# Windowed attention and an MLP on one core: both score tiles of a pair moved next to another pair's value products, five PSUM banks shared in turn

## The chip, the cores and the metric

One core of a Trainium2 chip runs the whole program in one launch. The metric is device time in microseconds (us) of one execution; a profiled execution also leaves a trace of every instruction on TensorE (PE, with its weight loads as PEld), VectorE (DVE), ScalarE (ACT), GpSimd (POOL) and the DMA queues.

## The reference

The inputs have batch 2, 8 heads, 768 positions and head dimension 64. Attention keeps the first four keys and a window of 128; its output feeds an MLP (512 to 2048 to 512) with a clipped quadratic gate; a last stage adds experts for tokens whose score is positive.

```
scores = scale * np.matmul(q, k.transpose(0, 1, 3, 2))
keep = is_sink | in_window
scores = np.where(keep, scores, -1000000000.0)
a = np.exp(scores - np.max(scores, axis=-1, keepdims=True))
a = a / (np.sum(a, axis=-1, keepdims=True) + 1e-09)
x = np.matmul(a, v)            # then heads side by side: 1536 tokens x 512
h = x @ w_in                   # float64 weights
g = np.where(h >= 1, h, np.where(h <= -1, 0.0, (h + 1) ** 2 / 4))
y = g @ w_out
```

## The kernel before

**Work.** A unit is one head over 256 queries (two tiles of 128); two heads make a pair, so there are 48 units and 24 pairs, 12 per batch. A pair goes through these steps, each with its engine:

- `trans_q`, `trans_k` (lines 304, 331): PE transposes of queries and keys into one bank each, which ACT copies out (lines 307, 334; in batch 1 lines 310, 336, and DVE then subtracts for a low part).
- `score(u, t)` (line 366): for query tile t the products of both heads. Each head has 64 rows, so the two heads lie in the upper and the lower half of the array (the trace writes 64*128) and run at the same time. Batch 0 has one part in full precision, batch 1 three parts in a faster format. Then per head DVE adds the mask and takes the maximum (line 370, `negmax`), which frees the bank, and ACT takes the exponential (line 374).
- `norm(u)` (lines 381 to 400): POOL, a reciprocal on DVE, four scalings (ACT for the first seven pairs, line 389, DVE after, line 391), small copies on POOL.
- `ptrans(n)` (line 417): PE transposes of one unit's weights, copied out by ACT (`pth`, line 421); `ptrans_sinks(u)` (line 429) for the four sink keys (`psk`, line 430).
- `av(u)` (lines 443, 446): the value products; each head writes 64 columns (128*64 in the trace), the sinks go first in the full array. ACT and DVE copy them out as `xh` and `xl` (lines 451, 452).

**The MLP between them.** From step 10 on, "pieces" of the MLP's first part fill PE between the attention steps: a piece is six matmuls of `h_mm` (line 467, tile `ph`) or three of `y_mm` (line 529, tile `y`). One unit of the MLP is four `h` pieces into one bank `ph`, of which there is only one. When its last piece is done, ACT takes a Relu (line 481) and a Square (line 482), DVE a minimum (line 487), which frees the bank, then ACT writes `gh` (line 489) and DVE `gl` (line 495). Between the last `h` piece of a unit and the first of the next, two `y` pieces stand. The last `y` of a group also has a copy out (`mr`, ACT line 554 and DVE line 552).

**Order.** PE's order is written by hand: for each step `s_` a string is read letter by letter. `a` and `b` are a pair's first and second score tile (`b` also the norm), `q` and `k` the transposes, `P` and `s` the transposes of weights and sinks, `A` the value products, and each dot a share of the step's pieces (three pieces a step). A period of two steps handles one pair. The other engines' order is chosen when the program is built; each works strictly in that order.

**Banks.** PSUM has eight: two for `y`, one for `ph`, two for score tiles (`pss`) and three (`pst`) in turn for transposes and value products. In the second half of the program (`behind`) the MLP alone remains.

Of the kernel before, what the change touches and what calls it, by code (L numbers as in the profile page):

```python
# [8 lines left out]
F32 = mybir.dt.float32  # L9
# [6 lines left out]
PSUM = bass.MemoryType.PSUM  # L16
# [8 lines left out]
def attention_moe_skip_kernel(  # L25
# [19 lines left out]
    P = 128  # L45
# [18 lines left out]
    psy = ctx.enter_context(tc.tile_pool(name="psy", bufs=1, space=PSUM))  # L64
    psh = ctx.enter_context(tc.tile_pool(name="psh", bufs=1, space=PSUM))
    pctx = ctx.enter_context(ExitStack())
    pss = pctx.enter_context(tc.tile_pool(name="pss", bufs=2, space=PSUM))
    pst = pctx.enter_context(tc.tile_pool(name="pst", bufs=3, space=PSUM))
    psz = None


# [27 lines left out]
    for i in range(2):  # L99
        a, b = mask[i][:, 0:P], mask[i][:, P + SK:]  # L100
# [166 lines left out]
    NPR = NU // 2  # L267
    natqk, pr_ = {}, [dict() for _ in range(NPR)]

    def geo(n):  # L270

        b, g, h = units[n]
        return b, g, h, ([2 * g + 1, 2 * g] if g % 2 else [2 * g, 2 * g + 1]), (0 if g % 2 else 1)
# [66 lines left out]
    def span_of(n, t):  # L340

        g = units[n][1]
        if g == 0:
            return (P + SK, P, first) if t == 0 else (P + SK, W, early)
        return ((t + g) % 2) * (P + SK), W, mask[g % 2]

    def score(u, t):

        b, g, h, _, _ = geo(2 * u)
        qt = pr_[u]["qt"]  # L350
        if t == 0:
            pr_[u].update(pr=ap.tile([P, 2, 2, W], F32, name="pr", bufs=2), lsum=ap.tile([P, 4], F32, name="lsum", bufs=2))
        pr, lsum = pr_[u]["pr"], pr_[u]["lsum"]
        c0, w, m = span_of(2 * u, t)
        scs = [pss.tile([P, 512], F32, name="sc") for j in range(2)]
        q_, k_ = slice(P * t, P * t + P), slice(c0, c0 + w)
        if b == 0:
            kt = ktf[h // 2]
            parts = [(qt[:, q_], kt[:, k_])]
        else:  # L360
            kt = kts[h // 2]
            parts = [(qt[:, x, q_], kt[:, y, k_]) for x, y in ((0, 0), (0, 1), (1, 0))]
        for n, (qq, kk) in enumerate(parts):
            for j in range(2):
                r = slice(D * j, D * j + D)
                nc.tensor.matmul(scs[j][:, :w], qq[r], kk[r], start=(n == 0), stop=(n == len(parts) - 1))  # L366
        for j in range(2):
            mi = (b * H + h + j) * (S // P) + 2 * g + t
            a = pr[:, j, t, :w]
            nc.vector.tensor_tensor_reduce(  # L370
                out=a, in0=scs[j][:, :w], in1=m, scale=-0.125, scalar=BIG,
                op0=ALU.add, op1=ALU.min, accum_out=negmax[:, mi:mi + 1],
            )
            nc.scalar.activation(  # L374
                a, a, AF.Exp, bias=negmax[:, mi:mi + 1], scale=-1.0, accum_out=lsum[:, 2 * j + t:2 * j + t + 1])

    def norm(u):
        g = units[2 * u][1]
        pr, lsum = pr_[u]["pr"], pr_[u]["lsum"]
        rs = ap.tile([P, 4], F32, name="rs", bufs=2)  # L380
        nc.gpsimd.tensor_scalar(out=rs, in0=lsum, scalar1=1e-9, scalar2=None, op0=ALU.add)
        nc.vector.reciprocal(rs, rs)
        for j in range(2):
            for t in range(2):
                w = span_of(2 * u, t)[1]
                a, r = pr[:, j, t, :w], rs[:, 2 * j + t:2 * j + t + 1]
                if u < 7:

                    nc.scalar.activation(a, a, AF.Copy, scale=r)  # L389
                else:  # L390
                    nc.vector.tensor_scalar(out=a, in0=a, scalar1=r, scalar2=None, op0=ALU.mult)
        if g:

            pc = pcs[u % 2]
            for j in range(2):
                c = SK * j
                dst = pc.rearrange("p t (x c) -> p t x c", x=9)[:, :, 0::8, c:c + SK]
                src = pr[:, j, :, P:P + SK]
                nc.gpsimd.tensor_copy(dst, src.unsqueeze(2).to_broadcast([P, 2, 2, SK]))
                nc.gpsimd.tensor_tensor(  # L400
                    out=pc[:, :, 32 + c:32 + c + SK], in0=src, in1=pc[:, :, c:c + SK].bitcast(F32), op=ALU.subtract)
# [280 lines left out]
    def prepare(s_):  # L682

        un = (s_ + 1) // 2 + 2
        upto("qk", un // 2 + 2, NU // 4, load_qk)
        if s_ >= 0:
            upto("v", (s_ // 2 + 1) // 2 + 1, NU // 4, load_v)
        return un
# [12 lines left out]
    with tc.manual_schedule(engines={mybir.EngineType.PE}):  # L701
        for s_ in range(-1, NU + 1):
            un = prepare(s_)
            before = done["p"]
            if s_ == -1:
                for t in ktf:
                    nc.gpsimd.tensor_copy(t[:, P + SK + P:2 * (P + SK)], zero[:, 0:SK])
                for t in kts:
                    nc.gpsimd.tensor_copy(t[:, :, P + SK + P:2 * (P + SK)], zero[:, 0:SK].unsqueeze(1).to_broadcast([P, 2, SK]))
                for t in pcs:  # L710
                    nc.gpsimd.memset(t.bitcast(F32), 0.0)
            if s_ == 3:
                raw_to(2)
                sinks(0)
            if s_ == NU // B + 3:
                sinks(1)
            np_ = npieces[s_] if s_ >= 0 else 0
            if s_ >= 0:
                convert_to(conv_for(sum(npieces[:s_ + 5])))
            if s_ < 0:  # L720
                for u in range(un - 1):
                    trans_q(u)
                    trans_k(u)
                done["tq"] = done["tk"] = un - 1
                score(0, 0)

            order = ("aAPs", "bqkAPs", "..a..A...Ps", "..b.qk.APs.")[s_ % 2 + 2 * (s_ >= 9)]
            dots, dot = order.count("."), 0
            for what in order:
                if what == ".":  # L730
                    a, b = np_ * dot // dots, np_ * (dot + 1) // dots
                    dot += 1
                    for i in range(b - a):
                        pieces[done["piece"]]()
                        done["piece"] += 1
                elif what == "q":
                    upto("tq", done["tq"] + 1, NPR, trans_q)
                elif what == "k":
                    upto("tk", done["tk"] + 1, NPR, trans_k)
                elif what == "a" and s_ // 2 + 1 < NPR:  # L740
                    score(s_ // 2 + 1, 0)
                elif what == "b" and (s_ + 1) // 2 < NPR:
                    score((s_ + 1) // 2, 1)
                    norm((s_ + 1) // 2)
                elif what == "P":
                    upto("p", s_ + (s_ >= LAG), NU, ptrans)
                elif what == "s":
                    upto("ps", (s_ + (s_ >= LAG)) // 2, NPR, ptrans_sinks)
                elif what == "A":
                    upto("av", before // 2, NPR, av)  # L750

        bad = const.tile([P, 1], F32, name="bad")
        ext = const.tile([P, 4], U32, name="ext")
        nc.sync.dma_start(ext[:, 0:2], n_sink.bitcast(U32).unsqueeze(0).to_broadcast([P, 2]))
        nc.sync.dma_start(ext[:, 2:4], window.bitcast(U32).unsqueeze(0).to_broadcast([P, 2]))
        extf = const.tile([P, 4], F32, name="extf")
        nc.vector.tensor_copy(extf, ext)
        sel = const.tile([P, 6], F32, name="sel")
        for i, val in enumerate((SK, 0, P, 0)):
            nc.vector.tensor_scalar(out=sel[:, i:i + 1], in0=extf[:, i:i + 1], scalar1=float(val), scalar2=None, op0=ALU.not_equal)  # L760
        nc.vector.tensor_reduce(out=bad, in_=negmax, axis=AX.X, op=ALU.max)
        nc.vector.tensor_scalar(out=sel[:, 4:5], in0=bad, scalar1=1.0e8, scalar2=None, op0=ALU.is_gt)
        actx.close()
        pctx.close()
        pst = ctx.enter_context(tc.tile_pool(name="pst1", bufs=1, space=PSUM))
        zctx = ctx.enter_context(ExitStack())
        psz = zctx.enter_context(tc.tile_pool(name="psz", bufs=1, space=PSUM))
        wp2 = wctx.enter_context(tc.tile_pool(name="wp2", bufs=8))
        wsk = wp2.tile([P, DM], F32, name="wsk", bufs=1)
        nc.sync.dma_start(wsk, w_skip.unsqueeze(0).to_broadcast([P, DM]))  # L770

        E_ = mybir.EngineType
        with tc.manual_schedule(engines={E_.DVE, E_.Activation, E_.Pool, E_.SP}):
            behind()
# [3 lines left out]
    pss = ctx.enter_context(tc.tile_pool(name="pss1", bufs=2, space=PSUM))  # L778
# [270 lines left out]
```

## Time and profile before

| what | us |
|---|---|
| median of three runs | 413.43 (411.69 to 414.58) |
| the profiled execution: its own time | 414.2 |
| the profiled execution: span of the trace | 412.4 |
| PE busy, share of the span | 382.7, 93% |
| DVE busy | 256.0, 62% |
| ACT busy | 221.1, 54% |

The page is read in three stretches: up to about 58 us the attention alone, then to about 216 us attention with pieces of the MLP between, then the MLP alone. The profiled execution is 0.77 us above the median.

### The profile page before, as it was taken

How to read it: one execution, taken by the hardware profiler on the slowest of the kernel's cores; microseconds unless marked ns; L12 is line 12 of the kernel's file. 1: busy time of each engine (PE TensorE's matmuls, PEld its weight loads, DVE VectorE, ACT ScalarE, POOL GpSimd, SP SyncE). 2: the span in 40 equal slices, each digit the busy share in tenths (PEclk: the TensorE clock that was granted, in tenths of full speed). 3: DMA queues.
4: the chain of work that ended last, by engine and by line, in shares of the span. 5: the costliest groups of instructions: out<-in, count | busy, mean ns of one | idle time of the engine just before them, and what ended most of it. 6: DMA issues, size and time to landing. Idle time of an engine off the chain costs nothing.

```text
span 412.4 us, 7126 instructions
## 1 busy us (share of the span) xinstructions
PE 382.7 (93%) x2548; PEld 317.9 (77%) x2548; DVE 256.0 (62%) x688; ACT 221.1 (54%) x542; POOL 30.4 (7%) x132
## 2 busy tenths in 40 slices
PE   4866869999999999999999999999999999999990
PEld 2543657777778777877788799999999999999980
DVE  1689963445656665555536897787837865454572
ACT  4779975566666667667544554444533333333320
POOL 5101210000101011000100000000000000000000
PEclk9999889999999999999999999999999999999997
DMA  8779671305124023110001664453525875976112
GB/s 182 180 229 242 191 206 25 79 0 142 38 54 117 7 60 102 27 27 25 29 26 52 201 208 161 144 150 106 154 102 180 292 270 184 298 255 208 52 76 86
DMA packets 65580, 53.31 MB, mean 129 GB/s; under 512 B 40320, under 2 KB 56704, under 8 KB 65536
## 3 DMA queue, kind: packets, MB, share of 16 engines
q1 hardware_dynamic: 64448, 52.51, 42.7%
q8 instruction: 22, 0.36, 0.4%
q10 hardware_dynamic: 1088, 0.26, 0.3%
q14 instruction: 22, 0.18, 0.1%
HBM read 46.47 MB, written 6.29 MB: 128 GB/s over the span
## 4 chain that ended last, share of the span: by engine, by line
PE 79%; DVE 8%; ACT 5%; DMA 3%; issue 2%; SPq 1%; POOL 0%; ACTq 0%; DVEq 0%
PE ph L467 21%; PE y L529 18%; PE z L529 12%; PE pt L467 11%; PE sc L366 6%; PE pt L446 5%; PE pt L417 3%; ACT pr L374 2%; PE pt L304 2%; DMA ext<-in_window_dram 1%; DVE pr L370 1%; DMA raw<-in_moe_w_in_dram 1%; DVE mt L487 1%; PE pt L331 1%; PE pt L429 1%
## 5 line engine op out<-in xcount | busy, mean ns | idle before, releaser
L467 PE MATMUL ph<-xh,wi 128*128 128x256 f32 x504 | 97.0, 291 | 3.9 <-DVE mt L487 3.9
L467 PEld LDWEIGHTS ph<-xh,wi 128*128 128x128 f32 x504 | 78.2, 189 | 9.8 <-DVE mt L487 4.1
L529 PE MATMUL y<-wo,gh 128*128 128x512 f32 x224 | 73.7, 410 | 1.3 <-ACT mr L554 1.3
L467 PE MATMUL ph<-xl,wi 128*128 128x256 f32 x252 | 70.9, 281 | 0.0
L374 ACT ACTIVATE pr<-pr,negmax 128x260 f32<-128x260 f32 (+1 forms) x96 | 46.8, 488 | 24.9 <-DVE negmax L370 24.3
L495 DVE TENSOR_TENSOR gl<-mt,gh 128x512 fp32r<-128x512 f32 x47 | 32.5, 692 | 28.2 <-ACT gh L489 27.9
L529 PE MATMUL z<-wo,gh 128*128 128x512 f32 x160 | 49.2, 389 | 0.0
L467 PEld LDWEIGHTS ph<-xl,wi 128*128 128x128 f32 x252 | 48.2, 191 | 0.0
L467 PE MATMUL pt<-xh,wi 128*128 128x256 f32 x264 | 47.3, 281 | 0.0
L489 ACT ACTIVATE gh<-mt 128x512 fp32r<-128x512 f32 x47 | 29.6, 630 | 32.0 <-PE z L529 13.2
L529 PEld LDWEIGHTS y<-wo,gh 128*128 128x128 f32 x224 | 37.7, 188 | 9.3 <-issue 2.4
L529 PE MATMUL y<-wo,gl 128*128 128x512 f32 x112 | 43.9, 392 | 0.0
L467 PEld LDWEIGHTS pt<-xh,wi 128*128 128x128 f32 x264 | 41.5, 188 | 1.3
L481 ACT ACTIVATE mt<-ph,half 128x512 f32<-128x512 f32 x31 | 21.2, 684 | 35.5 <-PE ph L467 35.5
L370 DVE CUSTOM_DVE_ANT_0 pr<-sc,mask 128x260 f32<-128x260 f32 x64 | 25.3, 423 | 23.9 <-PE sc L366 23.8
L487 DVE SCALAR_TENSOR_TENSOR mt<-ph,mt 128x512 f32<-128x512 f32 x31 | 21.3, 689 | 29.1 <-ACT mt L482 29.0
L467 PE MATMUL pt<-xl,wi 128*128 128x256 f32 x132 | 37.1, 281 | 0.0
L421 ACT ACTIVATE pth<-pt 128x512 f32<-128x512 f32 (+1 forms) x48 | 26.7, 556 | 16.4 <-PE pt L417 16.4
L417 PE MATMUL pt<-ident,pr 128*128 128x128 f32 x176 | 30.0, 291 | 3.3 <-ACT pr L389 1.7
L529 PEld LDWEIGHTS z<-wo,gh 128*128 128x128 f32 x160 | 28.7, 188 | 4.8
L529 PE MATMUL z<-wo,gl 128*128 128x512 f32 x80 | 31.1, 389 | 0.0
L482 ACT ACTIVATE mt<-mt 128x512 f32<-128x512 f32 x47 | 29.7, 632 | 1.0
(111 smaller groups left out, 573.7 us busy)
## 6 DMA issues: line engine op xcount, KB each, us to landing
raw<-in_moe_w_in_dram SPq DMA_DIRECT2D x32, 512.0 KB
raw<-in_moe_w_out_dram SPq DMA_DIRECT2D x32, 512.0 KB
vall<-in_v_dram SPq DMA_DIRECT2D x24, 128.0 KB
ypart<-mr SPq DMA_DIRECT2D x12, 256.0 KB
qn<-in_q_dram SPq DMA_DIRECT2D x22, 128.0 KB
kn<-in_k_dram SPq DMA_DIRECT2D x22, 128.0 KB
yi<-ypart SPq DMA_DIRECT2D x6, 256.0 KB
out_dram<-mr SPq DMA_DIRECT2D x6, 256.0 KB
```

The costliest lines, as they stand in the source:

```text
L366: nc.tensor.matmul(scs[j][:, :w], qq[r], kk[r], start=(n == 0), stop=(n == len(parts) - 1))
L370: nc.vector.tensor_tensor_reduce(out=a, in0=scs[j][:, :w], in1=m, scale=-0.125, scalar=BIG, op0=ALU.add, op1=ALU.min, accum_out=negmax[:, ...
L374: nc.scalar.activation(a, a, AF.Exp, bias=negmax[:, mi:mi + 1], scale=-1.0, accum_out=lsum[:, 2 * j + t:2 * j + t + 1])
L417: nc.tensor.transpose(pt[:, P * i:P * i + P], pr[:, t, c:c + P], ident)
L421: nc.scalar.activation(pr["pth"][:, n % 2, :w], pt[:, :w], AF.Copy)
L467: nc.tensor.matmul(ph, wih[f + i][:, wx, c * P:c * P + P], xx[gi][:, c], start=(c == 0 and x == 0), stop=(c == KC - 1 and x == 2),)
L481: nc.scalar.activation(t, ph, AF.Relu, bias=half, scale=0.5)
L482: nc.scalar.activation(t, t, AF.Square)
L487: nc.vector.scalar_tensor_tensor(out=t, in0=ph, scalar=1.0, in1=t, op0=ALU.max, op1=ALU.min)
L489: nc.scalar.activation(gh, t, AF.Copy)
L495: eng.tensor_tensor(out=gl, in0=t, in1=gh.bitcast(F32), op=ALU.subtract)
L529: nc.tensor.matmul(ycur[gi, tt], gg[:, c:c + P], woh[f + i][:, wx], start=(u == us[0] and i == 0 and x == 0), stop=(u == us[-1] and i == 1 ...
```

## The change

The order strings put both score tiles of the next pair and its norm at one place, right behind the value products of an earlier pair (`A` then `a`); `b` is gone. The two pools of banks become one of five, from which score tiles, transposes and value products take the next bank in turn. No instruction is added or removed on any engine. Lines after the pools stand one lower in the changed file (366 is 365).

```diff
-    pss = pctx.enter_context(tc.tile_pool(name="pss", bufs=2, space=PSUM))
-    pst = pctx.enter_context(tc.tile_pool(name="pst", bufs=3, space=PSUM))
+    pst = pctx.enter_context(tc.tile_pool(name="pst", bufs=5, space=PSUM))
...
-        scs = [pss.tile([P, 512], F32, name="sc") for j in range(2)]
+        scs = [pst.tile([P, 512], F32, name="pt") for j in range(2)]
...
-                score(0, 0)
-
-            order = ("aAPs", "bqkAPs", "..a..A...Ps", "..b.qk.APs.")[s_ % 2 + 2 * (s_ >= 9)]
+                for t in range(2):
+                    score(0, t)
+                norm(0)
+
+            order = ("AaPs", "qkAPs", "...Aa....Ps", "...qk..APs..")[s_ % 2 + 2 * (s_ >= 9)]
...
                 elif what == "a" and s_ // 2 + 1 < NPR:
-                    score(s_ // 2 + 1, 0)
-                elif what == "b" and (s_ + 1) // 2 < NPR:
-                    score((s_ + 1) // 2, 1)
-                    norm((s_ + 1) // 2)
+                    for t in range(2):
+                        score(s_ // 2 + 1, t)
+                    norm(s_ // 2 + 1)
```

PE, at the end of step 17 and the start of step 18 (the value products of the ninth pair, number 8), before: transposes of weights and sinks, one `y` piece, the first score tile of pair 10 (two heads), one `y` piece, the value products, then `h` pieces. The second score tile stands a step later.

```order
L417 MATMUL pt<-ident,pr 128x128 x4
L429 MATMUL pt<-ident,pc_148 72x128 x2
L529 MATMUL y_776<-wo,gh 128x512 x2
L529 MATMUL y_776<-wo,gl 128x512
L366 MATMUL sc<-ktf_141,qtf 128x260 x2
L529 MATMUL y_777<-wo,gh 128x512 x2
L529 MATMUL y_777<-wo,gl 128x512
L443 MATMUL pt<-psk,vsk 128x256
L446 MATMUL pt<-pth,vall 64x256 x2
L446 MATMUL pt<-pth,vall 64x128 x4
L467 MATMUL ph<-xh_125,wi 128x256 x2
```

The same place now:

```order
L416 MATMUL pt<-ident,pr 128x128 x4
L428 MATMUL pt<-ident,pc_145 72x128 x2
L528 MATMUL y_792<-wo,gh 128x512 x2
L528 MATMUL y_792<-wo,gl 128x512
L528 MATMUL y_793<-wo,gh 128x512 x2
L528 MATMUL y_793<-wo,gl 128x512
L442 MATMUL pt<-psk,vsk 128x256
L445 MATMUL pt<-pth,vall 64x256 x2
L445 MATMUL pt<-pth,vall 64x128 x4
L365 MATMUL pt<-ktf_138,qtf 128x260 x4
L466 MATMUL ph<-xh_122,wi 128x256 x2
```

The two `y` pieces now stand together, and all four score matmuls follow the value products directly.

ACT, from the value products of pair 8 on, before: two exponentials stand ahead of the copy `xh`, then Relu, a copy of transposed weights, Square, the copy `mr`, and the exponentials of the second score tile one by one later.

```order
L374 ACTIVATE pr,lsum<-pr,negmax 128x260 x2
L451 ACTIVATE xh_126<-pt 128x256
L481 ACTIVATE mt<-ph,half 128x512
L421 ACTIVATE pth<-pt 128x512
L482 ACTIVATE mt<-mt 128x512
L554 ACTIVATE mr<-y_776 128x512
L374 ACTIVATE pr,lsum<-pr,negmax 128x260
L307 ACTIVATE qtf<-pt 128x256
L334 ACTIVATE ktf_142<-pt 128x2x128
L489 ACTIVATE gh<-mt 128x512
L374 ACTIVATE pr,lsum<-pr,negmax 128x260
```

Now:

```order
L450 ACTIVATE xh_123<-pt 128x256
L373 ACTIVATE pr,lsum<-pr,negmax 128x260 x4
L480 ACTIVATE mt<-ph,half 128x512
L420 ACTIVATE pth<-pt 128x512
L481 ACTIVATE mt<-mt 128x512
L553 ACTIVATE mr<-y_792 128x512
L306 ACTIVATE qtf<-pt 128x256
L333 ACTIVATE ktf_139<-pt 128x2x128
L420 ACTIVATE pth<-pt 128x512
L488 ACTIVATE gh<-mt 128x512
L429 ACTIVATE psk<-pt 72x256
```

All four exponentials now stand in a row between the copy of the value products and the Relu that begins the release of the bank `ph`.

## Rows read from the trace of the kernel before

**Rows 1.** Three stretches: length, busy us (instructions) PE, PEld, DVE, ACT, POOL, clock, DMA.

```profile
0.00:58.00 58.00, 40.38 (x204) 25.30 (x205) 42.59 (x131) 44.69 (x133) 12.85 (x51) 0.97 0.78 206
58.00:216.00 158.00, 156.69 (x1151) 123.77 (x1151) 85.31 (x303) 99.72 (x286) 17.54 (x82) 0.99 0.21 54
216.00:412.40 196.40, 185.67 (x1198) 168.83 (x1196) 128.05 (x255) 76.72 (x124) 0.00 (x0) 0.99 0.52 167
```

**Rows 2.** PE's waits from 58 to 216 us: total us, times, longest.

```profile
PE ph L467 <- DVE mt L487: 3.9, 3, 3.2
```

**Rows 3.** PE's waits up to 58 us, same columns.

```profile
PE sc L366 <- DVE negmax L370: 4.1, 4, 2.6
```

**Rows 4.** Timeline around one score block: start, us, engine, line, tiles, idle before.

```profile
65.61 0.71 PE L366 MATMUL sc<-ktf,qtf 64*128 64x260 f32 x4
66.25 0.20 PEld L304 LDWEIGHTS pt<-ident,qn 128*128 128x128 f32 x2 [0.34 <-issue]
```

**Rows 5.** Timeline of PE around another score block, between pieces.

```profile
77.16 0.39 PE L467 MATMUL ph<-xh,wi 128*128 128x256 f32 x2
77.39 0.28 PE L467 MATMUL ph<-xl,wi 128*128 128x256 f32 x1
77.59 0.71 PE L366 MATMUL sc<-ktf,qtf 64*128 64x260 f32 x4
78.23 0.50 PE L467 MATMUL ph<-xh,wi 128*128 128x256 f32 x2
78.57 0.28 PE L467 MATMUL ph<-xl,wi 128*128 128x256 f32 x1
```

**Rows 6.** Timeline around the value products of one pair.

```profile
70.54 1.09 PE L446 MATMUL pt<-pth,vall 128*64 128x256 f32 x12
71.57 0.30 PEld L467 LDWEIGHTS ph<-xh,wi 128*128 128x128 f32 x2 [0.18 <-issue]
71.60 0.47 PE L467 MATMUL ph<-xh,wi 128*128 128x256 f32 x2
...
71.91 0.28 PE L467 MATMUL ph<-xl,wi 128*128 128x256 f32 x1
```

**Rows 7.** Timeline of PE over the period from pair 8's value products to pair 9's.

```profile
87.94 0.28 PE L443 MATMUL pt<-psk,vsk 72*128 72x256 f32 x1
...
89.16 0.50 PE L467 MATMUL ph<-xh,wi 128*128 128x256 f32 x2
...
90.54 0.28 PE L467 MATMUL ph<-xl,wi 128*128 128x256 f32 x1
...
91.89 0.71 PE L366 MATMUL sc<-ktf,qtf 64*128 64x260 f32 x4
...
94.29 0.48 PE L467 MATMUL ph<-xh,wi 128*128 128x256 f32 x2
...
96.61 0.28 PE L443 MATMUL pt<-psk,vsk 72*128 72x256 f32 x1
```

**Rows 8.** Timeline of ACT in that period.

```profile
90.86 0.69 ACT L481 ACTIVATE mt<-ph,half 128x512 f32<-128x512 f32 x1 [1.20 <-PE ph L467]
91.44 0.59 ACT L421 ACTIVATE pth<-pt 128x512 f32<-128x512 f32 x1
91.92 0.63 ACT L482 ACTIVATE mt<-mt 128x512 f32<-128x512 f32 x1
92.44 0.60 ACT L554 ACTIVATE mr<-y 128x512 f32<-128x512 f32 x1
93.10 0.51 ACT L374 ACTIVATE pr<-pr,negmax 128x260 f32<-128x260 f32 x1
```

**Rows 9.** Timeline of DVE in that period.

```profile
92.63 0.43 DVE L370 CUSTOM_DVE_ANT_0 pr<-sc,mask 128x260 f32<-128x260 f32 x1 [2.51 <-PE sc L366]
...
92.98 0.69 DVE L487 SCALAR_TENSOR_TENSOR mt<-ph,mt 128x512 f32<-128x512 f32 x1
```

**Rows 10.** The page's costliest groups: busy us, mean ns of one, idle before.

```profile
L374 ACT ACTIVATE pr<-pr,negmax 128x260 f32<-128x260 f32 (+1 forms) x96 | 46.8, 488 | 24.9 <-DVE negmax L370 24.3
```

## The prediction

> **What bounds the kernel now.** I read the stretches first, then the waits, then the timeline of PE. From 58 to 216 us PE is busy 156.69 of 158.00 us, DVE 85.31 and ACT 99.72 [rows 1]: in that middle stretch the sum of PE's own work sets the time, and its only waits of weight are three for the bank `ph`, 3.9 us together, of which the first alone is 3.2 [rows 2]. Up to 58 us no engine is full (PE 40.38, DVE 42.59, ACT 44.69 of 58) and PE waits for others, 4.1 us of it for a score bank that DVE has not yet freed [rows 3]. From 216 us on the MLP runs alone, PE 185.67 of 196.40 us busy; the change does not touch that part, so it should move as a whole with the end of the middle stretch.
>
> What the middle stretch can gain is hidden in "busy": matmuls of different shape do not follow each other as closely as equal ones. After a score block PE's weight loads stand still for 0.34 us before the next one starts, and the next load begins only 0.64 us after the block did [rows 4]. Around another block: equal `ph` matmuls follow at 0.23 us for two, so 0.12 each; from the last of them to the block are 0.20 us, so 0.08 too much; the block takes 0.64 to the next matmul; and the first two of those take 0.34 instead of 0.23, because their weights were not loaded ahead [rows 5]. Each change of shape so costs about 0.08 to 0.10 us of emptying and 0.10 of a weight load in the open, some 0.19. The value products show the same at their end: 0.18 us without a weight load, and 0.31 for the first two `ph` matmuls [rows 6].
>
> **The change part by part.**
>
> *Changes of shape.* Before, a pair has three islands between full-array work: score tile 0, score tile 1, value products, so six changes. Now value products and both score tiles are one island with three: into 128*64, on to 64*128, and out. Three are saved, 3 x 0.19 = 0.57 us. As a check I rebuild the period of [rows 7], from pair 8's value products at 87.94 us to pair 9's at 96.61, 8.67 us. Two isolated score blocks cost 2 x (0.08 + 0.64 + 0.11) = 1.66 us; a second block right behind the first costs only its streaming, 0.64 - 0.08 - 0.11 = 0.45, and the first shares its entry with the exit of the value products, which saves one change, 0.19. That is 0.83 + 0.45 - 0.19 = 1.09, so 0.57 saved; a little goes because one exit used to lead into short transposes, whose first load costs less. I take 0.52 per pair. Batch 1 has three short parts in place of one, with the same changes of shape, so I take the same. Pairs 7 to 23 have their scores in the middle stretch, 17 x 0.52 = 8.8 us.
>
> The step from value products to score tiles (128*64 to 64*128) has no row here. If it cost nothing, 0.19 more would go per pair, 0.71 in all, 12.1 us; if it cost twice a change, 0.33 and 5.6 us. I take one full change, since every change in the rows costs one, whichever shapes it joins. The Trainium skill (TensorEngine Tiling (Array Packing), Key Properties) says that changing the tiling mode drains TensorE while changing the tile does not; by it this step is a change too, and the sum is the 8.8 us, not 12.1.
>
> *Banks.* A period takes ten tiles from five banks, so each tile always meets the same predecessor: the four score tiles those of the `q` and `k` transposes, the second `P` and the sinks, and `q`, `k`, `P`, `s` those of the four score tiles. The predecessors of the score tiles must be copied out anyway before the value products and scores that stand there can run; the score tiles are read by DVE half a period before their banks are wanted. So the sharing costs nothing in the middle stretch as long as DVE's passes (line 370, the next work 0.35 us after one [rows 9]) run on time; without that cover `q` would wait on `negmax`.
>
> *Four exponentials in a row.* ACT works strictly in order, and an exponential takes 0.49 us [rows 10]. Once in four periods (pairs 8, 12, 16, 20 as value products) a unit of `h` pieces closes right behind the merged island, and the Relu that starts the release of `ph` is queued behind the four; behind it wait Square, DVE's minimum, and then PE. I walk pair 8 from the start of its value products. They take 1.22 us (87.94 to 89.16), the score tiles 1.09 to 2.31, twelve `h` matmuls 0.10 + 1.41 (two pieces), closing at 3.8. Before, PE came back for `ph` 3.6 us after the closing (90.54 + 0.12 to 94.29 [rows 7]), with one score block in between; without it and its extra switches, 0.8 less, so at 3.8 + 2.8 = 6.6. DVE passes the first score tile 0.74 us after the block starts (91.89 to 92.63) [rows 7, 9] and the exponential follows 0.47 later (93.10) [rows 8]; with 0.1 for the copy of the value products ahead on DVE, the four run from 1.22 + 1.3 = 2.5 to 4.5. Relu 0.58, `pth` 0.48, Square 0.63 [rows 8], minimum 0.69 [rows 9] and an estimated 0.15 of signals make 7.0. PE waits 0.4. At pairs 16 and 20 ACT's new order has `mr` (0.60) ahead of Square, so 1.0 there; at pair 12 I take 0.4 again. That is 2.8 us, and 0.7 for the late `pth` and `psk` that the next value products need: 3.5 us. From both sides: nothing, if the wait stays under the cover of `y` pieces, or 8 if the `mr` order and longer queues cost 2 us each.
>
> *The early stretch.* Score tile 1 and the norm come a step earlier, which helps; but a score tile now can wait for a bank that ACT must free. The 3.2 us wait at its end rests on the chain Relu, Square, minimum behind ACT's norm and four exponentials; I count it longer, and the second score tile, already done by then, pays it back (0.7 to 0.8 us of PE). Zero, with 3 us to either side, near the size of that wait and of the 4.1 us [rows 2, 3].
>
> *Sum.* 414.2 - 8.8 + 3.5 + 0 = 408.9 against the profiled execution, which lies 0.77 above the median: 408.1 us.
>
> **Rivals.**
>
> *Only the gain.* The waits for `ph` stay covered, because the two `y` pieces and transposes behind the island are enough, or because the four exponentials start earlier than I count. For it: my walk misses by only 0.4 us at two of the four places. Against: ACT's printed order has the Relu behind the exponentials. It gives 413.4 - 8.8 = 404.6; with the free step from value products to scores, about 402.
>
> *The evacuation takes it back.* Each island leaves five banks at once to ACT and DVE, and PE then waits not at four but at most of the 14 closings after the first, and for `psk` too. The Trainium skill (TensorEngine Tiling (Array Packing), PSUM Bottleneck) says that tiling speeds up TensorE but not the evacuation of PSUM. For it: between the sinks' transposes and the value products stand now only two `y` pieces, where a score block also stood. Against: ACT and DVE have over a third of the stretch free [rows 1]. At 0.5 us at each of 14 places it is 7 us, so 413.4 - 8.8 + 7 = 411.6.
>
> *Slower: one ring in the early stretch.* There PE, too, is often waited for, and a score tile whose bank waits for ACT's copy holds up all that PE has queued behind: transposes for the next pair, which DVE and ACT need to go on. Before, score banks waited for DVE alone, four times, 2.6 us at the longest [rows 3]. If pairs 1 to 6 each waited that 2.6 us on ACT, it would be 15.6 us against the 5.3 net gain: 423; it decides from 0.9 us a pair. Half of it, 1.6 us a pair, gives 417.7. Against: those copies are needed before the scores anyway.
>
> **How the numbers follow.** A difference of 1%, 4 us, is about what a measurement of this kernel can tell from none. Forecast 0.45 (408.1), only the gain 0.20 (404.6), evacuation 0.23 (411.6), slower 0.12 (417.7). One per cent faster is 409.3: of the forecast I put 0.36 below and 0.09 above, so faster 0.36 + 0.20 = 0.56, same 0.09 + 0.22 = 0.31, slower 0.13 with a hundredth of the evacuation. The range runs from the gain with the free step, 402, to just under the slower case, 415.5, which leaves out most of that case and the ends of the bounds.
>
> **What would show it.** In the new trace: a period of about 8.15 us from value products to value products where nothing waits; one score block of eight matmuls about 1.1 us long directly behind the twelve value products; waits of PE for `ph` in four places of 0.4 to 1.0 us, right after pairs 8, 12, 16 and 20, with the Relu behind four exponentials. No PE wait for score banks after 58 us. I am wrong if the step into the score tiles shows no gap or a longer one, if `ph` or `psk` waits sum to much more than 4 us, or if the middle stretch starts more than 3 us away from 58 us.

## The result, and the profile after

The changed kernel takes 409.58 us, median of four runs (409.18 to 410.68), beside 414.0 for the kernel before in the same comparison. The ratio is 0.9913 with a 95% interval of 0.9887 to 0.9938: 4.4 us or 0.9% faster. The forecast was 408.1, 1.5 us lower; the time lies inside the range. The gain is real, but a little under the 1% from which the prediction counted "faster" (0.56); by that line the case is "same", which had 0.31. The profiled execution took 409.3 us, its span is 407.5.

The three stretches after, as in [rows 1]: busy time of PE, weight loads, DVE, ACT and POOL, then the granted clock of PE, the DMA share and GB/s.

```profile
0.00:58.00 58.00, 35.72 (x202) 23.78 (x202) 41.50 (x130) 43.25 (x130) 14.19 (x54) 0.85 0.72 194
58.00:216.00 158.00, 152.54 (x1196) 129.51 (x1197) 86.13 (x308) 104.48 (x293) 15.92 (x78) 0.98 0.23 59
```

The early stretch has less PE work done and a lower clock (0.85). The cuts at 58 and 216 us no longer fall at the same work, so I cut the difference by work instead. PE's rows at the first value products after the `h` pieces begin (pair 5), in the middle, and at the first matmul of the MLP alone; columns are start, duration, engine, line, tiles, shape, count:

```profile
80.09 0.28 PE L442 MATMUL pt<-psk,vsk 72*128 72x256 f32 x1
80.30 1.09 PE L445 MATMUL pt<-pth,vall 128*64 128x256 f32 x12
81.32 1.15 PE L365 MATMUL pt<-ktf,qtf 64*128 64x260 f32 x8
82.39 0.74 PE L528 MATMUL y<-wo,gh 128*128 128x512 f32 x2
...
88.22 0.28 PE L442 MATMUL pt<-psk,vsk 72*128 72x256 f32 x1
...
209.74 0.44 PE L466 MATMUL pt<-xh,wi 128*128 128x256 f32 x2
```

From pair 7 to pair 8 the period is 8.13 us, and the eight score matmuls hold PE from 81.32 to 82.39, 1.07 us, directly behind the twelve value products. Pair 5 starts at 63.51 us (60.73 before), and the MLP alone at 209.74 (215.25 before). So the early stretch lost 2.8 us, the middle one went from 154.5 to 146.2 us, 8.3 less, and the end (197.2 before, 197.8 after) gave back 0.6: together the 4.9 us between the two spans. The 0.6 lies wholly behind the last instruction of the program's work, which ends at 405.5 us before and at 400.1 after; from the start of the MLP alone to there it is 190.3 us in both.

Where PE waits after, up to 58 us and from there to 216 us (what waited, for what; total, times, longest), to be held against [rows 2, 3]:

```profile
PE pt L303 <- DVE negmax L369: 7.1, 2, 4.3
PE pt L442 <- ACT psk L429: 2.1, 1, 2.1
```

```profile
PE ph L466 <- DVE mt L486: 8.8, 4, 6.2
```

The first row is the new ring at work: a transpose of queries now stands behind a score bank that DVE has not read yet, which before could only hold up a score tile. The wait for `ph` comes four times: 6.23 us before pair 5, then 0.27, 1.12 and 1.14 us behind pairs 8, 16 and 20. At pair 12, where two of the four exponentials are over 128 columns and follow each other by 0.4 instead of 0.5 us, no wait is left, and no score tile waits for a bank after 58 us. A row of the kernel before that stands beside [rows 2] is gone as well: PE's transposes of sinks waiting for a bank that DVE still had to read.

```profile
PE pt L429 <- DVE qt L311: 0.6, 3, 0.2
```

The 6.23 us, on PE, on ACT and on DVE of the changed kernel:

```profile
54.17 0.38 PE L428 MATMUL pt<-ident,pc 128*72 128x128 f32 x2
60.78 0.79 PE L466 MATMUL ph<-xh,wi 128*128 128x256 f32 x2 [6.23 <-DVE mt L486]
63.51 0.41 PE L442 MATMUL pt<-psk,vsk 72*128 72x256 f32 x1
```

```profile
53.35 0.51 ACT L373 ACTIVATE pr<-pr,negmax 128x260 f32<-128x260 f32 x1
...
54.91 1.72 ACT L388 ACTIVATE pr<-pr,rs 128x260 f32<-128x260 f32 x4 [0.32 <-DVE rs L381]
...
58.06 0.69 ACT L480 ACTIVATE mt<-ph,half 128x512 f32<-128x512 f32 x1
...
59.37 0.63 ACT L481 ACTIVATE mt<-mt 128x512 f32<-128x512 f32 x1
```

```profile
60.04 0.69 DVE L486 SCALAR_TENSOR_TENSOR mt<-ph,mt 128x512 f32<-128x512 f32 x1 [1.56 <-ACT mt L481]
```

PE reaches 54.17 us with one score tile more done than before: in the kernel before it issued the same transposes at 54.13. Up to there the early stretch had lost nothing. Then the Relu starts at 58.06, behind four exponentials, four norm passes and copies; before it started at 54.53. The exponentials are done before PE has to wait, so what holds the Relu here is the norm, a short wait of its own for DVE, and the copies. And the granted clock from 60.0 to 64.2 us is 0.50, the lower of the two levels, after PE had stood idle: twelve `ph` matmuls take 2.73 us (60.78 to 63.51), where six at the full clock take 0.69.

### The profile page after: what moved, and what is told of

It reads as the page before. It is cut to its first block, busy times and chain, and to the rows that moved or that the text cites. A ratio compares the mean times of both kernels' runs of the same rounds, so it can differ in the third digit from the quotient of the medians.

```text
span 407.5 us, 7136 instructions
## 1 busy us (share of the span) xinstructions
PE 368.4 (90%) x2548; PEld 316.8 (78%) x2548; DVE 253.6 (62%) x688; ACT 222.0 (54%) x542; POOL 30.1 (7%) x132
## 4 chain that ended last, share of the span: by engine, by line
PE 75%; ACT 8%; DVE 7%; DMA 4%; issue 3%; POOL 1%; SPq 1%; ACTq 0%; DVEq 0%; POOLq 0%
PE ph L466 20%; PE y L528 18%; PE z L528 12%; PE pt L466 11%; PE pt L445 5%; PE pt L365 4%; PE pt L416 3%; ACT pr L373 3%; DMA ext<-in_window_dram 1%; DMA raw<-in_moe_w_in_dram 1%; ACT pr L388 1%; PE pt L303 1%; DVE mt L486 1%; PE pt L330 1%; DVE cc L175 1%
## 5 line engine op out<-in xcount | busy, mean ns | idle before, releaser
L486 DVE SCALAR_TENSOR_TENSOR mt<-ph,mt 128x512 f32<-128x512 f32 x31 | 21.4, 689 | 37.5 <-ACT mt L481 37.5
L416 PE MATMUL pt<-ident,pr 128*128 128x128 f32 x176 | 28.6, 282 | 1.2 <-ACT pr L388 1.0
L480 ACT ACTIVATE mt<-pt,half 128x512 f32<-128x512 f32 x16 | 11.0, 687 | 29.6 <-PE pt L466 29.6
```

The lines of the kernel that those rows point to most:

```text
L416: nc.tensor.transpose(pt[:, P * i:P * i + P], pr[:, t, c:c + P], ident)
L480: nc.scalar.activation(t, ph, AF.Relu, bias=half, scale=0.5)
L486: nc.vector.scalar_tensor_tensor(out=t, in0=ph, scalar=1.0, in1=t, op0=ALU.max, op1=ALU.min)
```

## The experiments

The theory after the result: the middle stretch gains by saved changes of shape, about 0.19 us each, and loses by stalls for `ph` where a unit closes with its Relu queued behind four exponentials; the early loss is the first stall for `ph`. Rivals: the gain is that of the free use of the banks; the early loss comes from the ring, or from the order. Times are to be held against the changed kernel's 409.6 us; ratios are to the kernel before.

**Only the banks.** Before's order, one ring of five.

```diff
-    pss = ...bufs=2 / pst = ...bufs=3
+    pst = ...bufs=5
-        scs = [pss.tile(... name="sc") ...]
+        scs = [pst.tile(... name="pt") ...]
```

> The kernel before with one thing changed: the score tiles too are taken from one ring of five banks; PE's order is that of before. Theory (the gain is saved changes of shape, sharing costs nothing in the middle stretch): no gain; the period of an undisturbed pair stays at 8.67 to 8.95 us, the time is 414 us if the ring is harmless in the early stretch, and up to 417 if the ring is what starts the middle stretch 2.8 us late. Rival (the gain comes from the freer use of the banks): 409.6 us with a period near 8.15 us.

416.67 us, ratio 1.0083 (1.0058 to 1.0107): 0.8% slower. Pair 5, and pairs 9 and 10:

```profile
64.24 0.28 PE L442 MATMUL pt<-psk,vsk 72*128 72x256 f32 x1
...
99.46 0.28 PE L442 MATMUL pt<-psk,vsk 72*128 72x256 f32 x1
108.01 0.28 PE L442 MATMUL pt<-psk,vsk 72*128 72x256 f32 x1
```

The period is 8.55 us here and 8.68 at pairs 5 and 6, far from 8.15, so the bank rival falls as the main cause. But it doesn't fall whole. From pair 5 to the MLP alone this kernel takes 152.65 us (to 216.89), the kernel before 154.52. Of these 1.9 us, 0.9 lie in pair 5's period, which the kernel before ran in part at the lower clock (9.60 for 8.68). The other 1.0 lies in the three periods in which PE before waited for DVE's reading of `qt` (pair 9: 8.95 before, 8.55 here; 0.3 each at pairs 16 and 20). So the ring gives about 1 us of the middle stretch's 8.3. It costs the early stretch 3.5 us (64.24 for 60.73).

**Only the order.** The new order from step 10 on, old banks; the early steps as before.

```diff
-            order = ("AaPs", "qkAPs", "...Aa....Ps", "...qk..APs..")[...]
+            order = ("aAPs", "bqkAPs", "...Aa....Ps", "...qk..APs..")[...]
+            if s_ == 9:
+                order = "b" + order
```

> The changed order from step 10 on, but the early steps in the order of before, and two banks for scores and three for the rest throughout. Theory: the second score tile must wait until DVE has read the first; DVE starts 0.74 us after the block and takes 0.35 us for a bank, while PE wants the bank after 0.45 to 0.55, so 0.6 to 0.9 us of waiting per pair, 17 times: about 10 to 15 us, 417 to 422 us in all, with PE waits for the score pass of DVE at every pair. Rival (adjacency alone is enough, the shared banks don't matter): 407 us, no such waits.

434.08 us, ratio 1.0505 (1.0490 to 1.0520), 12 us beyond the expected 417 to 422.

```profile
86.39 0.71 PE L366 MATMUL sc<-ktf,qtf 64*128 64x260 f32 x4
87.83 1.38 PE L366 MATMUL sc<-ktf,qtf 64*128 64x260 f32 x4 [0.73 <-DVE negmax L370]
89.14 0.73 PE L529 MATMUL y<-wo,gh 128*128 128x512 f32 x2
```

The wait is of the expected size, but the second tile then takes 1.31 us (87.83 to 89.14) where it should stream in 0.45: its two heads get their banks one after the other, at 87.7 and 88.4 us, where DVE's two passes end. The period at pair 7 is 9.81 us (85.15 to 94.96), and pair 5 starts at 64.66 us, 3.9 later than before. The order is worth nothing without the banks; together they give the gain.

**A piece between value products and scores.**

```diff
-  "...Aa....Ps"
+  "...A..a..Ps"
```

> The changed kernel with one MLP piece put between the value products and the two score tiles, which stay next to each other. Theory (each change of shape costs 0.19 us whichever shapes it joins): one change more per pair, the period goes from 8.15 to 8.34 us, 17 pairs give 3.2 us: 412.8 us, less some tenths if the closing pieces get cover. Rival 1 (the step from value products to scores is as dear as going through the full array: only putting score tile next to score tile pays): 409.6 us. Rival 2 (this merging is worth two changes): 416 us.

422.39 us, ratio 1.0222 (1.0194 to 1.0251), much slower than any of the three.

```profile
81.50 0.28 PE L442 MATMUL pt<-psk,vsk 72*128 72x256 f32 x1
...
89.84 0.28 PE L442 MATMUL pt<-psk,vsk 72*128 72x256 f32 x1
...
98.45 0.47 PE L466 MATMUL ph<-xh,wi 128*128 128x256 f32 x2 [1.51 <-DVE mt L486]
...
165.66 0.77 PE L466 MATMUL ph<-xh,wi 128*128 128x256 f32 x2 [2.30 <-DVE mt L486]
```

The undisturbed period is 8.34 us: one change more costs 0.17 to 0.21, as the theory said. The rest is stalls: the exponentials now come a piece later, nearer to the closing, and the waits for `ph` behind pairs 8, 12, 16 and 20 grow to 1.51, 1.73, 2.30 and 2.30 us, 5.3 more in all. After the third wait the same two matmuls take 0.77 instead of 0.47 us; after the fourth they still take 0.48, but right behind them the clock falls too (0.63 from 202 to 206 us). The granted clock from 64 to 216 us is 0.97 where the changed kernel has 1.00, which is 0.03 x 152 = 4.6 us of PE. An estimate of 3.2 + 5.3 + 4.6 is 13.1. The start of the MLP alone moved by 12.6 us, and the spans differ by 13.2, 0.6 of it behind the last instruction.

**The early order of before, in the ring.** The diff is that of the order above, with the ring kept.

> The changed kernel with the order of before in the early steps (up to step 9), still in one ring of five banks. If the new order (both score tiles ahead of the transposes) is what starts the middle stretch 2.8 us late: first undisturbed value products near 60.7 us, 406.8 us in all. If it is the ring (transposes queue behind a score bank that DVE holds): 63.5 us as in the changed kernel, 409.6 us in all. The three stalls for the h bank after 90 us (2.5 us) stay in both cases.

413.98 us, ratio 1.0019 (1.0004 to 1.0034); pair 5 starts at 67.19 us.

```profile
50.03 0.58 PE L442 MATMUL pt<-psk,vsk 72*128 72x256 f32 x1 [4.20 <-ACT psk L429]
67.19 0.41 PE L442 MATMUL pt<-psk,vsk 72*128 72x256 f32 x1
```

Neither answer: going back to the old early order makes the start 3.7 us later, whether by that order itself or by the change-over at step 9. So nothing here says that the new order in the early steps is what costs.

**Scores ahead of the value products.**

```diff
-  "...Aa....Ps"
+  "...aA....Ps"
```

> The changed kernel with the two score tiles in front of the value products instead of behind them, still next to each other. The number of changes of shape is the same, and the four exponentials start some 1.0 us earlier. Theory (the stalls for the h bank right behind pairs 8, 16 and 20, 0.27 + 1.12 + 1.14 us, come from the Relu standing behind the four exponentials): the stalls go to nearly nothing, periods where nothing waits stay at 8.15 us, 407.2 us in all. Rival (the stalls come from the y copy and the Square, or from ACT being behind in general): stalls as before, 409.6 us. If the step from scores to value products costs something else than the reverse, the undisturbed period shows it: 0.19 us either way is 3.2 us.

404.57 us, ratio 0.9799 (0.9763 to 0.9834), 2.6 us less than expected.

```profile
59.80 2.10 PE L365 MATMUL pt<-ktf,qtf 64*128 64x260 f32 x8
...
77.48 1.15 PE L365 MATMUL pt<-ktf,qtf 64*128 64x260 f32 x8
78.56 0.38 PE L442 MATMUL pt<-psk,vsk 72*128 72x256 f32 x1
78.87 1.09 PE L445 MATMUL pt<-pth,vall 128*64 128x256 f32 x12
...
86.91 0.39 PE L442 MATMUL pt<-psk,vsk 72*128 72x256 f32 x1
```

No wait for `ph` is left after 58 us: PE is busy 158.00 of 158.00 us. That fits the Relu behind the exponentials, started 0.8 to 1.0 us too late. It doesn't part that from the rival of the `y` copy: at pairs 16 and 20 the changed kernel has `mr` ahead of Square on ACT and ahead of the minimum on DVE, and in this build `mr` stands behind both. The undisturbed period, too, is not as expected: 8.30 to 8.35 us. The sinks product (72*128, which follows a `y` piece without a gap in the changed kernel) now stands between 64*128 and 128*64 and makes one change more. Pairs 13 and 14, which have no sinks, have 7.19 and 7.20 us beside 7.17 and 7.18. With 15 such pairs the longer periods cost about the 2.5 us that the stalls give back. The spans differ by 5.6 us, and most of it comes from elsewhere: pair 5's island starts 3.7 us earlier (59.80 for 63.51), from there to the MLP alone it is 0.5 less (145.7 for 146.2), and 1.4 less remains behind the last instruction.

**The norm of pair 6 on DVE.**

```diff
-                if u < 7:
+                if u < 6:
```

> The changed kernel with the norm of pair 6, four passes, on DVE instead of ACT; PE's order is the same. Theory (the 6.2 us wait of PE for the h bank at 54.6 to 60.8 us is ACT's queue, in which the four norm passes, 1.7 us, stand ahead of the Relu): the wait falls to 4.0 to 4.5 us, the half clock behind it gets shorter too, 407 to 407.7 us in all. Rival (DVE's conversions set the wait; four passes more on DVE push its minimum back): the wait stays at 6 us or grows, 409.6 us or more.

409.15 us, ratio 0.9891 (0.9870 to 0.9912), not to be told from the changed kernel; the first wait is still 6.15 us.

```profile
56.76 1.14 DVE L390 TENSOR_SCALAR pr<-pr,rs 128x260 f32<-128x260 f32 x4
...
59.47 0.72 DVE L176 SCALAR_TENSOR_TENSOR cc<-raw,cc 128x512 uint32<-128x512 uint32 x1
60.11 0.68 DVE L486 SCALAR_TENSOR_TENSOR mt<-ph,mt 128x512 f32<-128x512 f32 x1
```

The rival holds: the minimum (L486) now stands behind the norm and conversion steps on DVE, and the Relu on ACT (57.81 for 58.06) behind copies that wait for conversions. Both queues are full there; to empty one moves the wait to the other.

**Each island one piece earlier.**

```diff
-  "...Aa....Ps"
+  "..Aa.....Ps"
```

> The changed kernel with no MLP piece between the head of the even step and the island: each island stands one piece earlier, so that the h unit that closed right behind the islands of pairs 8, 12, 16 and 20 closes one piece (six matmuls) later. Theory (those stalls are the time that the Relu waits behind four exponentials): one piece is 0.75 us for h and 1.4 for y, so the stalls of 0.27 and 1.1 us shrink to 0 and 0.4 or less, 407.4 to 408 us in all. Rival (whatever closes there waits for ACT's queue anyway, since the order on ACT moves too): 409.6 us, stalls as long as before or at other pairs.

427.74 us, ratio 1.0351 (1.0324 to 1.0378). I had walked only the four closings that stalled. They are covered now, but at pairs 7, 11, 15 and 19 the piece that closes a unit fell from ahead of the island to behind it, with only two `y` pieces before the next `h`:

```profile
PE ph L466 <- DVE mt L486: 10.1, 4, 2.8
PE pt L442 <- ACT psk L429: 2.0, 6, 0.5
```

(from 62 to 216 us, where the changed kernel has 2.5 us in all). The stall follows the closing, as the theory says; the edit was wrong. The clock is 0.97 again, from 64 to 216 us. These waits and that clock make some 14 of the 18 us; the rest is open. With the norm on DVE as well:

> The two edits together: the norm of pair 6 on DVE, and each island one MLP piece earlier. If the early wait and the stalls behind the islands are separate losses, their gains add up: 405 to 406 us. If the time that one gives back is lost in the other, no better than the better of the two alone, 407 us.

427.22 us, ratio 1.0324 (1.0299 to 1.0350): it tells nothing of addition, since neither edit alone gave back time.

**The sinks product last.** Scores first, and the sinks behind the value products, beside the `y` or `h` piece that follows:

```diff
-        if g:
-            nc.tensor.matmul(o[:, 0:256], vsk[b][:, h // 2], psk[0:72], start=True, stop=False)
...
-                    start=(i == 0 and g == 0), stop=(i == len(mm) - 1))
+                    start=(i == 0), stop=(i == len(mm) - 1 and g == 0))
+        if g:
+            nc.tensor.matmul(o[:, 0:256], vsk[b][:, h // 2], psk[0:72], start=False, stop=True)
```

> Scores in front of the value products as in the run before, and the product of the sinks (72*128, one matmul) behind the twelve value products of its pair instead of ahead of them. With scores first and the sinks ahead, pairs with sinks had an undisturbed period of 8.30 to 8.35 us, 0.17 more than in the changed kernel, and pairs without sinks had none more. Theory (PE pays 0.19 us whenever the shape changes, also into and out of the single sinks product between 64*128 and 128*64, and nothing where that product stands next to 128*128): the period goes back to 8.13 to 8.16 us, 15 pairs with sinks in the middle stretch give 2.7 us, 401.9 us in all. Rival (the 0.17 us is something else, such as the scores waiting for the transposes just ahead): 404.6 us.

```profile
77.22 1.09 PE L443 MATMUL pt<-pth,vall 128*64 128x256 f32 x12
...
84.27 1.15 PE L365 MATMUL pt<-ktf,qtf 64*128 64x260 f32 x8
85.34 1.09 PE L443 MATMUL pt<-pth,vall 128*64 128x256 f32 x12
86.36 0.39 PE L447 MATMUL pt<-psk,vsk 72*128 72x256 f32 x1
```

The period is 8.12 us, so the theory holds in the middle stretch; PE's last program instruction, and all behind it, is 3.5 us earlier than with the sinks first. Yet the time is 404.22 us, ratio 0.9782 (0.9748 to 0.9816), as good as the same and not the expected 401.9. In the two profiled executions the reason lies at the very end (below). The same edit on the changed kernel, where it puts the sinks between 128*64 and 64*128:

> The changed kernel (value products, then scores) with the sinks product moved behind the value products, so between 128*64 and 64*128. Theory: one change of shape more per pair with sinks and none per pair without; undisturbed period 8.32 us instead of 8.15, 15 pairs give 2.7 us, 412.3 us in all. Rival (where the single matmul stands costs nothing): 409.6 us.

```profile
78.79 1.09 PE L443 MATMUL pt<-pth,vall 128*64 128x256 f32 x12
79.81 0.38 PE L447 MATMUL pt<-psk,vsk 72*128 72x256 f32 x1
80.13 1.15 PE L365 MATMUL pt<-ktf,qtf 64*128 64x260 f32 x8
...
87.15 1.09 PE L443 MATMUL pt<-pth,vall 128*64 128x256 f32 x12
```

The period is 8.36 us, 0.2 more as expected, but the time is 409.45 us, ratio 0.9899 (0.9864 to 0.9933): the first `ph` wait is 4.8 instead of 6.2 us in this build, pair 5 starts 2.4 to 2.8 us earlier, and 1.1 us less remains behind the last instruction, which hides the 3 us. The total alone would have misled here.

**Pieces from step 9 on**, with scores first and sinks last (`START, LAG = 9, 8`).

> The same with the MLP pieces starting one step earlier, at step 9. Theory (the wait of 4.6 to 6.2 us for the h bank before pair 5 is the first unit's release standing behind DVE's conversions and ACT's exponentials and norm, where it ends up by the order of building): the first Relu and Square now stand ahead of the norm on ACT and the minimum ahead of four conversions on DVE, the wait falls to about half, 399 to 400.5 us in all. Rival (the work of DVE and ACT up to 58 us sets the start of the middle stretch, whatever PE does): first undisturbed value products near 62 us as before, 402 us.

412.52 us, ratio 0.9980 (0.9957 to 1.0003). The first wait is 4.39 us, not half. The shifted pieces also bring waits of 5.12 us for the load of batch 1's sinks (line 132, at 128.5 us) and of 0.2 to 1.2 us for `ph`. It settles nothing beyond the first number: Relu and minimum further ahead in their queues hardly shortened the wait (4.86 with step 10).

**Part of the conversions on GpSimd**, with scores first and sinks last.

```diff
-        lower(cf, t[:, 0], t[:, 1], nc.vector)
+        lower(cf, t[:, 0], t[:, 1], nc.gpsimd)
```

> Scores first and the sinks last, as before, and the last step of each weight conversion beside attention (the subtraction for the lower half, 0.68 us on DVE, twelve of them) on GpSimd, which is idle three quarters of the early stretch; nothing is left out. The first unit's minimum then has no conversion between it and the work before on DVE, and Relu and Square no conversion copies between them on ACT. Theory (PE's wait of 4.9 us before pair 5, and the 6.2 us in the changed kernel, is the release of the h bank queued behind conversions on DVE): the wait falls to 2 us or less, pair 5 starts at 57 to 59 us instead of 61.0, 400.5 to 402 us in all. Rival 1 (the exponentials and the norm on ACT set it): the wait stays at 4 us or more, 404 us. Rival 2 (GpSimd is so slow at it that weights come late): waits of PE for weights, more than 404 us.

410.38 us, ratio 0.9918 (0.9891 to 0.9945). The first `ph` wait falls to 2.7 us, but pair 5 starts at 69.33 us, because DVE gets slower elsewhere: two conversion steps on DVE, and the subtraction on POOL beside the second:

```profile
46.47 0.71 DVE L175 SCALAR_TENSOR_TENSOR cc<-raw,cc 128x512 uint32<-128x512 uint32 x1
47.22 1.80 DVE L176 SCALAR_TENSOR_TENSOR cc<-raw,cc 128x512 uint32<-128x512 uint32 x1
```

```profile
47.20 1.26 POOL L185 TENSOR_TENSOR wo<-cc,wo 128x512 fp32r<-128x512 f32 x1
```

The score passes behind them are late, and PE waits for these twice more, 3.5 and 3.7 us. That the first wait falls (4.9 to 2.7) fits DVE's queue as a part of it, but PE comes to it 10 us later here, when DVE's conversions are done in any case. The 2.7 that stay end with ACT's Square, which stands behind exponentials and norm. It looks as if the sum of DVE's and ACT's work sets the early stretch, and not one instruction's place; no run shows that by itself.

## Why the prediction came near, point by point

*Changes of shape: right.* 0.52 us per pair gave 8.8; the middle stretch lost 8.3 us net, with stalls for `ph` of 2.5 us where before it had 0.6, so about 10.2 gross. Not all of that is change of shape. About 0.6 is the clock: before, pair 5's value products ran at the lower level and took 1.80 us, after they take 1.18.

```profile
61.08 1.87 PE L446 MATMUL pt<-pth,vall 128*64 128x256 f32 x12
```

```profile
63.85 1.25 PE L445 MATMUL pt<-pth,vall 128*64 128x256 f32 x12
```

About 1.0 is the banks (the run with the ring alone). What is left, 8.5 us or 0.5 a pair, is the forecast saving, and where neither kernel waits the periods show it directly: 8.70 to 8.16 us from pair 6 to 7, 8.44 to 7.92 from pair 10 to 11. The undisturbed period of 8.13 to 8.16 us is the forecast 8.15, the score block 1.07 for 1.09. The open bound, the step from value products to scores, costs one full change: parting them added 0.17 to 0.21, and a 72*128 product put between them 0.2, while one next to a 128*128 matmul adds nothing (8.12 us). The Trainium skill (TensorEngine Tiling (Array Packing), Key Properties) says that a change of the tiling mode drains TensorE and a change of the tile does not. That a change of mode costs these runs bear out, at 0.17 to 0.21 us; no run here tries a change of the tile alone.

*Banks: harmless in the middle stretch, as forecast, but not without effect.* With the ring alone the period stays at 8.55 to 8.68 us and no score tile waits. The prediction counted only the waits for `ph` as of weight. The three waits for `qt`, 0.6 us by their row and 1.0 by the periods, are what the ring takes away, a gain that it did not have.

*Four exponentials in a row: right in mechanism and in sum.* Forecast 0.4, 0.4, 1.0, 1.0; measured 0.27, none, 1.12 and 1.14. The 0.9 us more at pairs 16 and 20 than at pair 8 goes with `mr` ahead of Square there, as forecast. With the scores first the stalls are gone (and `mr` has moved too); with later scores or closings behind the island they grow. The 0.7 us for late `pth` and `psk` did not come.

*The early stretch: the step that was mis-sized.* I took zero: the wait would be longer, and the second score tile would pay it back. The wait grew by 3.0 us (3.23 to 6.23), not by the 0.7 to 0.8 that the score tile pays back; the tile paid 0.63, and the lower clock behind the longer wait took 0.4. That is the 2.8 us. I had seen the chain Relu, Square, minimum, but I put the wait before behind ACT's norm and four exponentials; in that trace Relu starts at 54.53 and Square at 56.34, with an exponential and copies between, and the norm follows at 56.86. I had not seen that the builder would now set the norm's four passes (1.72 us) and the copies ahead of the Relu; ACT's printed order showed it. The exponentials end at 53.9, before the wait begins. Moving the norm to DVE did not shorten the wait, so its cause is not shown beyond the two full queues. The 3 us of range covered it.

*Sum.* -8.8 + 3.5 + 0 was forecast; -10.2 + 1.9 (stalls, more than before) + 2.8 + 0.6 at the end is -4.9. The gain was 1.4 us larger and the stalls 1.6 smaller than forecast, against 2.8 in the early stretch and 0.6 at the end, so that the profiled executions differ by 0.4 us less than forecast; the rest of the 1.5 us is how they lie to their medians. That it came so near is in part luck: the 1.6 us of clock and banks, which the forecast did not have, offset more than half of the early loss. The rival of a slow ring showed as 3.5 us in the run with the banks alone; in the changed kernel what queues behind the ring waits for DVE's score passes, not for ACT's copies as I had it. In that rival's price, half of 2.6 us a pair is 1.3 and not 1.6, which makes 415.9 and not 417.7; the forecast does not hang on it.

*What stays open.* Pair 5's value products start between 60.7 and 69.3 us in these builds, and no single edit explains it: ring, order and conversions each moved it, the norm did not, and what one queue gave the other took. Separate early banks with the new early order were not tried, nor was `mr` moved by itself.

## What to carry to other kernels

Where PE is the bound, count the changes of shape between neighbouring matmuls, small ones included, and order an island so that the odd product stands next to the full-array work; here that is 0.2 us each. Then follow what the moved work puts in front of other engines' releases: putting scores ahead of the value products starts the exponentials 1 us earlier and takes away the three stalls (404.6 us, ratio 0.980). Its 5 us are not the worth of that, though: the stalls' 2.5 us went into longer periods, and most of the rest is an earlier start and less time behind the last instruction. Judge such edits by the undisturbed period and the waits, since a start that shifts by 3 us from build to build hides, or feigns, a gain of the same size.

## What the runs showed of the hardware that was not expected

- After the last instruction of the program's work the span goes on for 6 to 9 us, differently in each profile. Below, the last such instruction with scores first and then with the sinks last: 6.1 and 9.0 us remain, which takes back 2.9 of the 3.5 us. No run tells why.

```profile
core 0 of [0], span 401.9 us
...
395.70 0.14 DVE L793 TENSOR_SCALAR anyi<-anyf 1x1 int32<-1x1 f32 x1
```

```profile
core 0 of [0], span 401.4 us
...
392.24 0.14 DVE L793 TENSOR_SCALAR anyi<-anyf 1x1 int32<-1x1 f32 x1
```

- A wait of PE can cost more than its length: with the piece between, after one wait of 2.30 us the next two matmuls ran at the lower level (0.77 us). After the other wait of 2.30 us they ran at the higher (0.48), and the clock fell behind them (0.63 from 202 to 206 us). After the waits of 1.51 and 1.73 us it stayed at the higher level.
- A subtraction on GpSimd slowed DVE's instruction beside it to 1.80 us; one of the same form just before took 0.71. The Trainium skill (GPSIMD Engine Reference, Specifications) says that GpSimd shares its SBUF interfaces with VectorE and contends with DVE instructions that have two SBUF inputs, among others. This instruction has two, and the trace agrees.
